# Centring-only LayerNorm with the deviation applied at eviction, and three changes of order, in a fused attention and MLP block

## The chip, the cores and the metric

The kernel runs on one core of one Trainium2 chip. The metric is the device time of one execution in microseconds (us), as a median over runs. The profile is taken on one such execution. Its time base is the "span", which runs from the first instruction to the end of the program; the device time is 1.7 to 2.0 us longer than the span in these runs. All runs of this study are in the fast state, with a granted TensorE clock between 0.998 and 1.000.

The engines are named as the profile names them: PE is TensorE (matmuls), PEld its weight loads, DVE is VectorE, ACT is ScalarE, POOL is GpSimd, and SP issues most of the DMAs.

## The reference

```python
# x: 2048 x 576, bf16; wqkv: 576 x 1728; wo: 576 x 576; w1: 576 x 4608; w2: 4608 x 576
def _layernorm(x, axis=-1, eps=1e-5):
    m = jnp.mean(x, axis=axis, keepdims=True)
    v = jnp.var(x, axis=axis, keepdims=True)
    return (x - m) / jnp.sqrt(v + eps)

# attention: 32 heads of 18; each row looks at 8 rows, two apart, ending at itself
h  = x + A(_layernorm(x), wqkv, wo)
h2 = h + gelu(_layernorm(h) @ w1 + b1) @ w2 + b2
```

What matters for this change is that the rows of a LayerNorm can be scaled after a matmul as well as before it: `((x - m) * rstd) @ W` is `((x - m) @ W) * rstd`, because `rstd` is one number for each row.

## The kernel before

The 2048 rows are 16 tiles of 128 rows. The even tiles are projected first. One projection of one tile onto Q, K or V is a "duo": a phase 0 of 10 matmuls and a phase 1 of 8, each of 64 rows by 288 columns. A "visit" does two duos (three where an output projection joins), and 24 visits do all of QKV. Attention itself is elementwise work on DVE. Then eight groups of two tiles go through MLP1 (GELU on ACT, straight out of PSUM) and MLP2. From the third group on, MLP2 uses sums of blocks of its two operands (made on DVE) to save matmuls.

Some words are used throughout. PSUM is the memory that PE writes; a "PSUM pair" is a buffer in it that ACT or DVE must empty (the "eviction") before PE may use it again. "Fillers" are matmuls whose results nobody uses, run before the first data have come. A "halo reload" reads K or V back from DRAM, shifted by rows, into `kv_ring`. `oT` is attention's output, `hnT` the second LayerNorm's output, both transposed by DMA through the buffer `td`; `w2b_sb` is the last part of `w2`.

The first LayerNorm of an even tile: statistics on DVE, the power on POOL, then the normalised tile on DVE. Only then can PE transpose it.

```python
def ln_stats(srcs, tag, c1, c0, bufs, first=None):
    # ... bn_stats on two halves, bn_aggr
    veps = sb.tile([P, n], F32, tag=f"{tag}_veps", name=f"{tag}_veps", bufs=bufs)
    nc.vector.tensor_scalar(out=veps[:], in0=mv[:, :, 1], scalar1=c1, scalar2=c0, op0=ALU.mult, op1=ALU.add)
    return mv, veps

def ln_rstd(veps, tag, bufs):
    rstd = sb.tile([P, n], F32, tag=f"{tag}_rstd", name=f"{tag}_rstd", bufs=bufs)
    nc.gpsimd.tensor_tensor(out=rstd[:], in0=veps[:], in1=mhalf[:].to_broadcast([P, n]), op=ALU.pow)
    return rstd
# ... cut: each group of tiles has a tag of its own here (ln1_0 to ln1_10), so no buffer is shared

def visit(makes, hook=None, between=(), early=False):
    duos, marks = [], []
    for make in makes:
        duos.append(make())
        marks.append(marker(phase(duos[-1], 0, None)))
        if hook and len(duos) == (1 if early else len(makes)):
            hook()                       # the transposes of the next two tiles
    for duo, mark in zip(duos, marks):
        phase(duo, 1, mark)
        duo["evac"]()                    # ACT empties the PSUM pair
        if duo is duos[0]:
            for fn in between:
                fn()

# ... cut: the eviction of a duo
pace[0] = nc.scalar.copy(out=dst..., in_=ps...).ins

# order of the start; after[v] is what the other engines are given after visit v
after = {
    0: [c_(ln1_sr, 3), c_(ln1_apply, 2), c_(ln1_apply, 3)],
    1: [c_(ln1_sr, 4), c_(ln1_sr, 5), c_(ln1_apply, 4), c_(ln1_apply, 5)],
    2: [c_(ln1_sr, 6), c_(ln1_sr, 7), c_(ln1_apply, 6), c_(ln1_apply, 7)],
    3: [c_(ln1_stats, 8)],               # statistics of the first four odd tiles
    # ... cut

# the first group: mid[0] runs between the two phases 1 of MLP1's first visit
mid[0] = [c_(exps, d)]                   # exp on ACT, between two table loads
ia[0] = [c_(wo_visit, (c, "B"))]         # first output projection, before MLP2's first row
ia[12] = [c_(exps, e), c_(wo_visit, (d, "A")), c_(ln2_pair, c, d, (e,)), ...]
```

## Time and profile before

| | before |
|---|---|
| median of the runs, four sets of rounds | 369.19 to 369.36 us |
| span of the profiled execution | 366.9 us |
| PE busy | 359.4 us, 98% |
| first QKV projection on PE | 7.38 us |
| statistics of the odd tiles start on DVE | 18.05 us |
| first MLP1 of group 1, of group 2, of group 8 | 69.32, 109.24, 329.66 us |

One caution for all that follows: the profiled execution of before took 368.69 us, which is about 0.6 us less than the medians. Every "lead" against this trace is therefore probably a little too small; leads of two changed kernels against each other are not touched by that.

The page of before. The first lines give the busy time of each engine and its share of the span; the second block is the busy share in tenths in 40 equal slices.

```profile
span 366.9 us, 11419 instructions
PE 359.4 (98%) x4900; PEld 295.5 (81%) x4900; DVE 299.3 (82%) x414; ACT 230.4 (63%) x514; POOL 41.3 (11%) x47
...
PE   8999999999999999999999999999999999999996
...
DVE  5899999999999999999989999989995699520331
...
PEclk9999999999999999999999999999999999999999
```

PE is full from the second slice on, and DVE is nearly full until about 275 us. The Trainium skill, page "Perfetto Trace Analysis", section "Identifying the Most-Contended Engine", says that the busy share of matmuls is not a good measure of how close PE is to its limit, because pipelined instructions look smaller. Here, too, the 98% doesn't show what the change can win. The list of PE's waits does: who was waited for, us in total, how often, and the longest.

```profile
PE busy L750 <- DVE prod L743: 1.5, 1, 1.5
PE po L557 <- ACT h_all L538: 0.8, 1, 0.8
PE pm L215 <- ACT h_all L538: 0.5, 1, 0.5
PE o_pt L182 <- DVE h L449: 0.4, 1, 0.4
PE po L642 <- DVE h_all L622: 0.2, 1, 0.2
PE pq L215 <- ACT kv_ring L301: 0.2, 1, 0.2
```

The first line only delays fillers. The next four are what parts 2 and 3 of the change aim at: ACT's GELUs before MLP2 (0.8) and in MLP1 (0.5), DVE's `h` before a transpose (0.4), a block sum of the last group (0.2). Together they are 1.9 us, and this is about the size of what can be won after the start.

The timeline of ACT in before, around the wait of 0.5 us: start, duration, engine, line, operation and tiles, and how many in a row.

```profile
73.31 0.84 ACT L538 ACTIVATE h_all<-pm,b_sb 128x256 bf16<-128x256 f32 x2
74.17 1.28 ACT L371 ACT_TABLE_LOAD   x1
75.47 0.42 ACT L371 ACTIVATE logits<-logits 128x256 f32<-128x256 f32 x1
75.90 1.28 ACT L514 ACT_TABLE_LOAD   x1
77.19 0.20 ACT L514 ACTIVATE warm<-mhalf 128x1 f32<-128x1 f32 x1
```

The exp takes 0.42 us, but with two table loads it keeps ACT from GELU, and so from emptying PSUM, from 74.17 to 77.39 us. For the later comparison, the timeline of DVE in before where the start ends:

```profile
17.50 0.41 DVE L166 TENSOR_SCALAR q_all<-x_all,ln_mv,ln_rstd 128x512 bf16<-128x512 bf16 x1 [0.22 <-POOL ln_rstd L162]
17.83 0.31 DVE L166 TENSOR_SCALAR xn_tail<-x_all,ln_mv,ln_rstd 128x128 bf16<-128x128 bf16 x1
18.05 0.81 DVE L151 BATCH_NORM_STATS2 ln_stats<-x_all 128x6 f32<-128x288 bf16 x2
```

In brackets stands the idle time before an instruction and what ended it. At 18.05 us DVE begins the statistics of the odd tiles.

### The profile page before, as it was taken

The numbers are of one execution on the slowest core, as the hardware profiler recorded it, in microseconds if no ns is written. First come the engines' busy times: TensorE is split into PE (matmuls) and PEld (weight loads), VectorE is DVE, ScalarE is ACT, GpSimd is POOL, SyncE is SP. The second block draws the span as 40 slices with busy tenths as digits, with TensorE's granted clock in tenths as the row PEclk, the third lists the DMA queues.
The fourth block names the chain that finished last, engine by engine and source line by source line (L and its number), as shares of the span: only waits on it lengthen the run. The fifth ranks groups of instructions, "written<-read, shape, count | busy, mean of one in ns | idle before, by whom it ended". The sixth has DMA issues, their size and how long they took to land.

```text
span 366.9 us, 11419 instructions
## 1 busy us (share of the span) xinstructions
PE 359.4 (98%) x4900; PEld 295.5 (81%) x4900; DVE 299.3 (82%) x414; ACT 230.4 (63%) x514; POOL 41.3 (11%) x47
## 2 busy tenths in 40 slices
PE   8999999999999999999999999999999999999996
PEld 3789877888778877887788778877887788779974
DVE  5899999999999999999989999989995699520331
ACT  2688755798638673568546865685568556726620
POOL 2322004000220031002100111011101010100000
PEclk9999999999999999999999999999999999999999
DMA  7989798954557625520553145305520452030001
GB/s 237 317 224 269 186 208 224 333 195 71 179 152 155 229 83 101 126 48 34 136 106 69 36 122 110 77 32 133 107 54 33 89 102 38 2 90 18 2 2 33
DMA packets 61891, 43.70 MB, mean 119 GB/s; under 512 B 31872, under 2 KB 60160, under 8 KB 61840
## 3 DMA queue, kind: packets, MB, share of 16 engines
q1 hardware_dynamic: 59952, 41.13, 41.2%
q0 software_dynamic: 1728, 1.77, 4.6%
q8 instruction: 38, 0.62, 0.7%
q10 hardware_dynamic: 160, 0.07, 0.1%
q14 instruction: 13, 0.11, 0.1%
HBM read 21.10 MB, written 12.42 MB: 91 GB/s over the span
## 4 chain that ended last, share of the span: by engine, by line
PE 78%; DVE 11%; ACT 6%; issue 1%; DMA 1%; POOL 1%; SPq 1%; DVEq 0%
PE pm L215 37%; PE po L642 22%; PE po L557 10%; PE pw L215 4%; PE pq L215 4%; ACT h_all L538 3%; DVE ln_stats L151 2%; DVE prod L339 2%; DVE prod L385 1%; DVE prod L333 1%; PE busy L750 1%; DMA hnT<-td 1%; DVE prod L391 1%; POOL ln_rstd L162 1%; DVE ln_mv L152 1%
## 5 line engine op out<-in xcount | busy, mean ns | idle before, releaser
L538 ACT ACTIVATE h_all<-pm,b_sb 128x256 f16<-128x256 f32 (+1 forms) x288 | 108.5, 498 | 73.2 <-PE pm L215 73.2
L215 PE MATMUL pm<-hnT,w_sb 64*128 64x256 bf16 x2304 | 143.0, 269 | 0.6 <-ACT h_all L538 0.5
L215 PEld LDWEIGHTS <-w_sb 64*128 64x128 bf16 x2304 | 114.2, 94 | 13.6 <-issue 2.5
L642 PEld LDWEIGHTS <-h_all 128*128 128x128 f16 x544 | 52.2, 98 | 15.8 <-issue 2.5
L215 PE MATMUL pq<-wq_sb,xnT 64*128 64x288 bf16 x768 | 54.2, 283 | 0.3 <-ACT kv_ring L301 0.2
L215 PEld LDWEIGHTS <-xnT 64*128 64x128 bf16 x864 | 43.9, 94 | 9.2 <-ACT xnT L262 0.6
L339 DVE TENSOR_TENSOR prod<-prod 128x2304 bf16<-128x2304 bf16 (+1 forms) x64 | 44.2, 691 | 2.1
L642 PE MATMUL po<-w2a_sb,h_all 128*128 128x288 bf16 (+1 forms) x312 | 43.6, 286 | 0.2 <-DVE h_all L622 0.2
L385 DVE TENSOR_TENSOR prod<-kv_ring,probs 128x4608 bf16<-128x4608 bf16 x16 | 40.9, 2555 | 2.4 <-DMA kv_ring<-kv_dram 2.1
L333 DVE TENSOR_TENSOR prod<-kv_ring,q_all 128x4608 bf16<-128x4608 bf16 x16 | 40.8, 2549 | 0.2
L215 PE MATMUL pm<-hnT,w1h_sb 64*128 64x256 bf16 x288 | 39.6, 269 | 0.0
L465 POOL TENSOR_TENSOR ln_rstd<-ln_var,mhalf 128x1 f32<-128x1 f32 x14 | 16.4, 1172 | 183.7 <-ACT ln_var L464 183.7
L557 PEld LDWEIGHTS <-h_all 128*128 128x128 bf16 x288 | 27.8, 98 | 8.8 <-issue 1.9
L391 DVE TENSOR_TENSOR prod<-prod 128x2304 bf16<-128x2304 bf16 (+1 forms) x32 | 33.8, 1057 | 1.0
L557 PE MATMUL po<-w2a_sb,h_all 128*128 128x288 bf16 x224 | 28.6, 286 | 0.8 <-ACT h_all L538 0.8
L642 PEld LDWEIGHTS <-kv_ring 128*128 128x128 f16 x240 | 23.4, 98 | 6.3 <-DVE kv_ring L622 0.4
L301 ACT CAST kv_ring<-pq 128x576 bf16<-128x576 f32 x32 | 19.4, 641 | 8.3 <-PE pq L215 8.2
L642 PE MATMUL po<-w2b_sb,h_all 128*128 128x288 bf16 (+1 forms) x152 | 22.2, 286 | 0.0
L622 DVE TENSOR_TENSOR kv_ring<-h_all 128x1536 f16<-128x1536 f16 (+2 forms) x8 | 6.6, 820 | 16.3 <-ACT h_all L538 16.3
L215 PE MATMUL pw<-wo_sb,oT 64*128 64x288 bf16 x256 | 19.5, 283 | 0.0
L162 POOL TENSOR_TENSOR ln_rstd<-ln_veps,mhalf 128x1 f32<-128x1 f32 (+2 forms) x13 | 13.2, 1019 | 49.0 <-DVE ln_veps L156 42.4
L449 DVE TENSOR_TENSOR h<-pw,x_all 128x576 f32<-128x576 f32 x16 | 11.5, 752 | 7.7 <-PE pw L215 7.7
(97 smaller groups left out, 370.7 us busy)
## 6 DMA issues: line engine op xcount, KB each, us to landing
w_sb<-in_B_w_dram SPq DMA_DIRECT2D x6, 768.0 KB, 5.6
kv_ring<-kv_dram SPq DMA_DIRECT2D x28, 144.0 KB, 2.7
w2a_sb<-in_B_w_dram SPq DMA_DIRECT2D x4, 1008.0 KB, 6.3
kv_dram<-kv_ring SPq DMA_DIRECT2D x13, 288.0 KB, 4.4
out_dram<-o_sb SPq DMA_DIRECT2D x15, 144.0 KB, 2.9
td<-q_all SPq DMA_DIRECT2D x14, 144.0 KB, 2.5
td<-hn SPq DMA_DIRECT2D x14, 144.0 KB, 1.8
x_all<-in_A_x_dram SPq DMA_DIRECT2D x12, 144.0 KB, 2.7
```

The costliest lines, as they stand in the source:

```text
L162: nc.gpsimd.tensor_tensor(out=rstd[:], in0=veps[:], in1=mhalf[:].to_broadcast([P, n]), op=ALU.pow)
L215: last = nc.tensor.matmul(duo["g"][r ^ swap][i], lhsT=lhsT, rhs=rhs, start=(swap == 0 and i == 0 and kt == 0), stop=(swap == 1 and kt == K ...
L301: pace[0] = nc.scalar.copy(out=dst.rearrange("p (d g h) -> p g d h", g=2, h=H // 2), in_=ps[:, :, 0:HALF].rearrange("p g (h d) -> p g d h" ...
L333: nc.vector.tensor_tensor(out=prod[:], in0=k_ring[j % 2], in1=q_all[:, j, :].unsqueeze(1) .to_broadcast([P, W, D]), op=ALU.mult)
L339: nc.vector.tensor_tensor(out=prod[:, :, o * H:o * H + n], in0=prod[:, :, a * H:a * H + n], in1=prod[:, :, c * H:c * H + n], op=ALU.add)
L385: nc.vector.tensor_tensor(out=prod[:].rearrange("p w (d h) -> p w d h", h=H), in0=v_ring[j % 2].rearrange("p w (d h) -> p w d h", h=H), in ...
L391: nc.vector.tensor_tensor(out=prod[:, 0:n, :], in0=prod[:, 0:n, :], in1=prod[:, n:2 * n, :], op=ALU.add)
L449: nc.vector.tensor_tensor(out=h[:].rearrange("p (g c) -> p g c", g=2), in0=pw[:, :, 0:HALF], in1=x_of(j).rearrange("p (g c) -> p g c", g=2 ...
L465: nc.gpsimd.tensor_tensor(out=rstd[:], in0=var[:], in1=mhalf[:], op=ALU.pow)
L538: pace[0] = nc.scalar.activation(out=hT(grp)[:, f, 0:N], in_=ps[:, r, i * N:(i + 1) * N], func=ACT.Gelu_apprx_tanh, bias=b1_sb[:, f:f + 1] ...
L557: nc.tensor.matmul(banks[half], lhsT=hT(grp)[:, f, i * P:(i + 1) * P], rhs=w2_rows(f)[:, half * HALF:(half + 1) * HALF], start=(f == 0), s ...
L642: nc.tensor.matmul(bank, lhsT=l, rhs=r, start=start, stop=stop, skip_group_check=True)
```

## The change

The intent has three parts.

1. **Start.** An even tile is only centred (one subtraction) before its transposes; `rstd` is computed later and handed to ACT as the scale of the PSUM eviction. The statistics of the second tile go to ACT. Fillers run on a constant, so that they need not wait for DVE. The transposes of two tiles, which stood together in a visit, are split: one tile behind each duo. The `eps` step of the even tiles gets one shared tag with two buffers. V's weights are loaded in two pieces, and their last rows through ACT's queue; the copy of one transposed tile goes from ACT to DVE.
2. **MLP1 of the first group.** The exp goes behind the second duo; the last visit empties the PSUM pair that MLP2 needs first; the first output projection moves into MLP1; one transpose of attention's output moves one phase later.
3. **Last groups.** The last LN2 is shared between ACT (one tile) and DVE (the other), and the block sums of `h` are made in pieces, the first of them during MLP1.

```diff
-    def visit(makes, hook=None, between=(), early=False):
+    def visit(makes, hook=None, between=(), late=None):
 ... a hook or a between may now be a dict {after which duo: functions}; late is a duo begun inside the last phase 1
-                pace[0] = nc.scalar.copy(out=..., in_=...).ins
+                scale = dict(scale=rstd_of[j]) if j in EVEN else {}
+                pace[0] = nc.scalar.activation(out=..., in_=..., func=ACT.Copy, **scale).ins
 ...
-            load_wqkv_half(nc.scalar, slice(1, 2))
+            load_wqkv_half((nc.scalar, nc.scalar), slice(1, 3))
-            load_wqkv(2)
-            load_wqkv_half(nc.sync, slice(2, 3))
+            load_wqkv(2, 0, 2)
+            load_wqkv(2, 2, KF)
-        for n in [512] * 9 + [P] * 5:
-            nc.tensor.matmul(busy[:, 0, 0:n], lhsT=prod[:, 0, 0:P], rhs=prod[:, 0, 0:n], start=True, stop=True)
+        ones = nc.const_aps.tensor(1.0, [P, 512], BF16)
+        for n in [512] * 8 + [P] * 5:
+            nc.tensor.matmul(busy[:, 0, 0:n], lhsT=ones[:, 0:P], rhs=ones[:, 0:n], start=True, stop=True)
 ...
+        def ln1_even(gi):
+            mv, veps = ln1[gi] = ln_stats([x_all[:, EVEN[gi], :]], f"ln1_{gi}", 1.0, EPS, 1, None, False)
+            center(EVEN[gi], mv[:, 0, 0:1], ALU.subtract)
+        def ln1_even_act(gi):            # second tile: two accumulating passes on ACT
 ...
+        def ln1_even_rstd(*gis):
+            for gi in gis:
+                mv, var = ln1.pop(gi)
+                veps = qp.tile([P, 1], F32, tag="ln1_veps", name="ln1_veps", bufs=2)
+                nc.vector.tensor_scalar(out=veps[:], ...)
+                rstd_of[EVEN[gi]] = ln_rstd(veps, f"ln1_{gi}", 1)[:, 0:1]
 ...
-            0: [c_(ln1_sr, 3), c_(ln1_apply, 2), c_(ln1_apply, 3)],
-            1: [c_(ln1_sr, 4), c_(ln1_sr, 5), c_(ln1_apply, 4), c_(ln1_apply, 5)],
-            2: [c_(ln1_sr, 6), c_(ln1_sr, 7), c_(ln1_apply, 6), c_(ln1_apply, 7)],
-            3: [c_(ln1_stats, 8)],
+            0: [c_(ln1_even, 3), c_(ln1_even, 4)],
+            1: [c_(ln1_even_rstd, 2, 3), c_(ln1_even, 5)],
+            2: [c_(ln1_even, 6), c_(ln1_even, 7), c_(ln1_even_rstd, 4, 5)],
+            3: [c_(ln1_even_rstd, 6, 7), c_(ln1_stats, 8)],
 ...
-            18: [c_(tr_o, A[1], "D")],
+            18: {1: [c_(tr_o, A[1], "D")]},
-                mid[0] = [c_(exps, d)]
+                mid[0] = {1: [c_(exps, d)]}
-                ia[0] = [c_(wo_visit, (c, "B"))]
+                late_wo = wo_duo(c, "B")
 ...
-                x["h"] += [c_(h_sums, SR, NM, (0, 2)), c_(h_sums, SR, NM, (1, 3))]
+                mid[3] = {1: [c_(h_sums, SR, 16)]}
+                x["h"] += [c_(h_sums, 16, NM)]
 ... and in group 7, ln2 of one tile on ACT, of the other on DVE
```

More of the change, by code (lines that the diff above doesn't have):

```diff
@@ L114, in load_wqkv, with load_wqkv_half @@
              A_wqkv[k0 * P:k1 * P, t * D:(t + 1) * D].rearrange("(k p) c -> p k c", p=P))
-    def load_wqkv_half(engine, ts):
+    def load_wqkv_half(engines, ts):
         src = A_wqkv[KF * P:D, :].rearrange("p (t g c) -> p t g c", t=3, g=2)
         for r in range(2):
-            engine.dma_start(out=wqh_sb[half_rows(r), ts, :], in_=src[:, ts, r, :])
+            engines[r].dma_start(out=wqh_sb[half_rows(r), ts, :], in_=src[:, ts, r, :])
     def load_wo(qs):
@@ L141, in load_w2, with ln_stats @@
         load(dst, B_w2[f0 * P:f1 * P, :].rearrange("(ft p) c -> p ft c", p=P))
-    def ln_stats(srcs, tag, c1, c0, bufs, first=None):
+    def ln_stats(srcs, tag, c1, c0, bufs, first=None, eps=True):
         n = len(srcs)
@@ L154, in ln_stats @@
                 first()
+        if not eps:
+            return mv, None
         veps = sb.tile([P, n], F32, tag=f"{tag}_veps", name=f"{tag}_veps", bufs=bufs)
@@ L227, in marker, with first @@
         return nop
-    def visit(makes, hook=None, between=(), early=False):
+    def visit(makes, hook=None, between=(), late=None):
         duos, marks = [], []
-        for make in makes:
+        def first(make):
             duos.append(make())
             marks.append(marker(phase(duos[-1], 0, None)))
-            if hook and len(duos) == (1 if early else len(makes)):
+        for make in makes:
+            first(make)
+            if hook and not isinstance(hook, dict) and len(duos) == len(makes):
                 hook()
-        for duo, mark in zip(duos, marks):
-            phase(duo, 1, mark)
-            duo["evac"]()
-            if duo is duos[0]:
-                for fn in between:
-                    fn()
+            elif isinstance(hook, dict) and len(duos) in hook:
+                hook[len(duos)]()
+        for n in range(len(makes) + (late is not None)):
+            if late is not None and n == len(makes) - 1:
+                first(late)
+            phase(duos[n], 1, marks[n])
+            duos[n]["evac"]()
+            for fn in (between.get(n, ()) if isinstance(between, dict) else between if n == 0 else ()):
+                fn()
     xnT, xn_tail = {}, {}
@@ L252, in tr_x @@
     def tr_x(js, tag):
-        pair = psum_pair(tag, "xt_pt", BF16)
+        pair = psum_pair(tag or "CAB"[(ring_pos[0] + 1) % 3], "xt_pt", BF16)
         for n, j in enumerate(js):
@@ L261, in copy @@
                 for k0, k1 in ((0, 2), (2, KT)) if j == EVEN[0] else ((0, KT),):
-                    nc.scalar.copy(out=xnT[j][:, k0:k1], in_=tr_view(pair, n)[:, k0:k1])
+                    copy = nc.vector.tensor_copy if j == EVEN[1] else nc.scalar.copy
+                    copy(out=xnT[j][:, k0:k1], in_=tr_view(pair, n)[:, k0:k1])
             copies.append(copy)
@@ L300, in evac @@
                 dst = (q_all[:, j, :], k_ring[j % 2][:, j // 2, :], v_ring[j % 2][:, j // 2, :])[t]
-                pace[0] = nc.scalar.copy(out=dst.rearrange("p (d g h) -> p g d h", g=2, h=H // 2),
-                                         in_=ps[:, :, 0:HALF].rearrange("p g (h d) -> p g d h", h=H // 2)).ins
+                scale = dict(scale=rstd_of[j]) if j in EVEN else {}
+                pace[0] = nc.scalar.activation(out=dst.rearrange("p (d g h) -> p g d h", g=2, h=H // 2),
+                                               in_=ps[:, :, 0:HALF].rearrange("p g (h d) -> p g d h", h=H // 2),
+                                               func=ACT.Copy, **scale).ins
                 if j == ATT_ORDER[0] and t > 0:
@@ L454, in ln2, with ln2_more @@
     def ln2(j):
-        h = ln2_h(j)
+        ln2_h(j)
+        ln2_more(j)
+    def ln2_more(j):
+        h = h_of[j]
         hn[j] = (h,) + ln_stats([h[:]], "ln2", 1.0 + EPS, EPS * EPS, 2)
@@ L472, in ln2_send, with ln2_out @@
         hn[j] = dma_out(y[:])
+    def ln2_out(j):
+        hn[j] = dma_out(hn[j][:])
     read = [None]
@@ L727 @@
     with tc.manual_schedule(engines={ENG.PE, ENG.Activation, ENG.DVE, ENG.SP, ENG.Pool}):
-        for i in range(2):
-            load_x(EVEN[i:i + 1])
+        load_x(EVEN[0:1])
+        load_x(EVEN[1:2])
         load_wqkv(1, 0, 2)
         load_wqkv(1, 2, KF)
-        load_wqkv_half(nc.scalar, slice(1, 2))
+        load_wqkv_half((nc.scalar, nc.scalar), slice(1, 3))
         load_x(EVEN[2:3])
         load_x(EVEN[3:4])
-        load_wqkv(2)
-        load_wqkv_half(nc.sync, slice(2, 3))
+        load_wqkv(2, 0, 2)
+        load_wqkv(2, 2, KF)
         load_x(EVEN[4:6])
@@ L740 @@
         load_wqkv(0)
-        load_wqkv_half(nc.sync, slice(0, 1))
+        load_wqkv_half((nc.sync, nc.sync), slice(0, 1))
         load_x(ODD[4:8])
@@ L762, in ln1_rstd @@
             ln1[gi] += (ln_rstd(ln1[gi][1], f"ln1_{gi}", 1),)
-        def ln1_apply(gi):
-            mv, _, rstd = ln1.pop(gi)
-            for i, j in enumerate(ln1_groups[gi]):
-                if j not in EVEN[5:]:
-                    ln_apply(q_all[:, j, :], x_all[:, j, :], mv[:, i, 0:1], rstd[:, i:i + 1])
-                    continue
-                ln_apply(q_all[:, j, 0:KF * P], x_all[:, j, 0:KF * P], mv[:, i, 0:1], rstd[:, i:i + 1])
-                xn_tail[j] = qp.tile([P, 2, HP], BF16, tag="xn_tail", name="xn_tail", bufs=3)
-                ln_apply(xn_tail[j][:], x_all[:, j, KF * P:D].unsqueeze(1).to_broadcast([P, 2, HP]),
-                         mv[:, i, 0:1], rstd[:, i:i + 1])
+        rstd_of = {}
@@ new lines, in center @@
+        def center(j, mean, op):
+            nc.vector.tensor_scalar(out=q_all[:, j, 0:D if j in EVEN[:5] else KF * P],
+                                    in0=x_all[:, j, 0:D if j in EVEN[:5] else KF * P], scalar1=mean, scalar2=None, op0=op)
+            if j in EVEN[5:]:
+                xn_tail[j] = qp.tile([P, 2, HP], BF16, tag="xn_tail", name="xn_tail", bufs=3)
+                nc.vector.tensor_scalar(out=xn_tail[j][:], in0=x_all[:, j, KF * P:D].unsqueeze(1).to_broadcast([P, 2, HP]),
+                                        scalar1=mean, scalar2=None, op0=op)
@@ new lines, in ln1_even @@
+        def ln1_even(gi):
+            mv, veps = ln1[gi] = ln_stats([x_all[:, EVEN[gi], :]], f"ln1_{gi}", 1.0, EPS, 1, None, False)
+            center(EVEN[gi], mv[:, 0, 0:1], ALU.subtract)
+        def ln1_even_act(gi):
+            j = EVEN[gi]
+            junk = q_all[:, ODD[-1], :]
+            nmean, var = (qp.tile([P, 1], F32, name=f"ln1_{t}") for t in ("nmean", "sq"))
+            nc.scalar.activation(out=junk, in_=x_all[:, j, :], func=ACT.Identity, scale=-1.0 / D, accum_out=nmean[:])
+            nc.scalar.activation(out=junk, in_=x_all[:, j, :], func=ACT.Square, bias=nmean[:], accum_out=var[:])
+            center(j, nmean[:], ALU.add)
+            ln1[gi] = (None, var)
@@ L775, in ln1_sr @@
+        def ln1_even_rstd(*gis):
+            for gi in gis:
+                mv, var = ln1.pop(gi)
+                veps = qp.tile([P, 1], F32, tag="ln1_veps", name="ln1_veps", bufs=2)
+                nc.vector.tensor_scalar(out=veps[:], in0=var[:] if mv is None else mv[:, 0, 1:2],
+                                        scalar1=1.0 / D if mv is None else 1.0, scalar2=EPS, op0=ALU.mult, op1=ALU.add)
+                rstd_of[EVEN[gi]] = ln_rstd(veps, f"ln1_{gi}", 1)[:, 0:1]
         def ln1_sr(gi):
@@ L789, in ln1_act @@
             ln_apply_act(q_all[:, j, :], x_all[:, j, :], rstd[:, i:i + 1], nmr[:, i:i + 1])
-        ln1_sr(0)
-        ln1_sr(1)
-        ln1_apply(0)
-        ln1_apply(1)
-        ln1_sr(2)
+        ln1_even(0)
+        ln1_even_act(1)
         A = ATT_ORDER
@@ L817, in ln2_stats @@
             for j in (c, d):
-                (add_b2 if c == GROUPS[-1][0] else put_b2)(j)
+                put_b2(j)
         def ln2_ins(c, d):
@@ L873 @@
         hooks = {
-            1: c_(tr_x, EVEN[2:4], "D"),
-            2: c_(tr_x, EVEN[4:6], "D"),
-            3: c_(tr_x, EVEN[6:8], "D"),
+            **{n: {m: c_(tr_x, EVEN[2 * n + m - 1:2 * n + m], "D" if m == 1 else None) for m in (1, 2)} for n in (1, 2, 3)},
             12: c_(tr_b1, "D"),
@@ L887 @@
         tr_x(EVEN[1:2], "C")
+        ln1_even_rstd(0, 1)
+        ln1_even(2)
         for qd in range(len(seq) // 2):
@@ L891 @@
                 duos.append(wo_duo(wo_with[qd], "D"))
-            visit(duos, hooks.get(qd), between.get(qd, ()), qd in (1, 2))
+            visit(duos, hooks.get(qd), between.get(qd, ()))
             call(after.get(qd, ()))
@@ L899, with mlp1_plan, mlp1 @@
         h_all = late.tile([P, FT, 2 * P], BF16, name="h_all")
-        def mlp1_plan(p, q, r, s, fast):
-            end = (r, s, p) if fast else (s, r, p)
+        def mlp1_plan(p, q, r, s, end):
             return [[([2 * v + n], tag) for n, tag in enumerate(tags)] for v, tags in enumerate(((p, q), (r, s), (p, q), end))]
-        def mlp1(grp, plan, ahead, between):
+        def mlp1(grp, plan, ahead, between, late=None):
             for v, duos in enumerate(plan):
                 call(ahead.get(v, ()))
-                visit([mlp1_duo(grp, us, tag) for us, tag in duos], None, between.get(v, ()))
+                visit([mlp1_duo(grp, us, tag) for us, tag in duos], None, between.get(v, ()), late if v == 3 else None)
         def mlp2_tile(grp, i, tag, inserts):
@@ L922, in exps, with wo_visit @@
             gelu_table()
-        def wo_visit(*duos):
-            visit([wo_duo(j, tag) for j, tag in duos], (lambda: [ahead[0]() for _ in range(2)]) if len(duos) == 1 else None)
+        def wo_visit(*duos, fill=False):
+            visit([wo_duo(j, tag) for j, tag in duos], (lambda: [ahead[0]() for _ in range(2)]) if fill else None)
         ROWS = {2: 8, 3: 12, 4: 12, 5: 12, 6: NM, 7: NM}
@@ L933 @@
             e, f = GROUPS[k + 2] if k + 2 < len(GROUPS) else (None, None)
-            m1, mid, ia, ib = {0: []}, {}, {}, {}
+            m1, mid, ia, ib, late_wo = {0: []}, {}, {}, {}, None
             if k in (1, 2):
@@ L938 @@
                 m1[0] += [c_(halos, 1), c_(att_qk_a, d), c_(att_qk_rest, d, 1), c_(halo, d, 1)]
-                mid[0] = [c_(exps, d)]
+                mid[0] = {1: [c_(exps, d)]}
                 m1[1] = [c_(pv_t, c), c_(pv_t, d), c_(load_w2, 4), c_(att_qk, e, 0)]
-                ia[0] = [c_(wo_visit, (c, "B"))]
-                ia[12] = [c_(exps, e), c_(wo_visit, (d, "A")), c_(ln2_pair, c, d, (e,)), c_(halos, 2), c_(send_o, e)]
+                late_wo = wo_duo(c, "B")
+                ia[12] = [c_(exps, e), lambda d=d: wo_visit((d, "A"), fill=True), c_(ln2_pair, c, d, (e,)), c_(halos, 2), c_(send_o, e)]
                 ib[0] = [c_(finish_out, g[0])]
@@ L955 @@
             if k < 2:
-                mlp1(g, mlp1_plan(p, q, r, s, False), m1, mid)
+                mlp1(g, mlp1_plan(p, q, r, s, (s, r, p) if k else (r, s, p)), m1, mid, late_wo)
                 mlp2_tile(g, 0, "D", ia)
@@ L985 @@
             if c is not None:
-                x["h"] = [c_(ln2_stats, c, d)] + x["h"]
-                x["6"] += [c_(ln2_send, c)]
-                x["7"] = [c_(ln2_send, d)] + x["7"]
+                if k == 6:
+                    x["h"] = [c_(ln2_h, c), c_(ln2_act, c), c_(ln2_h, d)] + x["h"] \
+                        + [c_(ln2_more, d), c_(ln2_rstd, d), c_(ln2_send, c), c_(add_b2, c), c_(add_b2, d), c_(ln2_bias, d)]
+                    x["6"] += [c_(ln2_hn, d), c_(ln2_out, d)]
+                else:
+                    x["h"] = [c_(ln2_stats, c, d)] + x["h"]
+                    x["6"] += [c_(ln2_send, c)]
+                    x["7"] = [c_(ln2_send, d)] + x["7"]
                 x["in"] = [c_(ln2_ins, c, d)] + x["in"]
                 wo = lambda tags: wo_visit((c, tags[0]), (d, tags[1]))
-            mlp1(g, mlp1_plan(p, q, r, s, True), m1, mid)
+            mlp1(g, mlp1_plan(p, q, r, s, (r, s, p)), m1, mid)
             mlp2_fast(g, rows, (p, q, r, s), wo, x)
```

## The prediction

> **What bounds the kernel now.** TensorE. The page's busy table gives PE 98% of the 366.9 us span; the window table gives PE 200.0 of 200 us between 110 and 310 us, and the granted clock is 1.00. The matmul stream is untouched, so only the places where PE waits or runs fillers can pay. The PE timeline and the wait list name them: before the first projection (7.38 us; fillers from 1.53 us), about 1 us inside the first QKV visit (7.38 to 10.57 us where a later visit of 36 matmuls takes 2.21 us), 0.35 us at 54.8 us (second o transpose waits for DVE's h), 0.47 us at 78.9 us (ACT was doing exp between two table loads instead of emptying a PSUM pair), 0.76 us at 89.3 us (ACT's last GELUs before MLP2), about 0.3 us at 319.5 us, 0.14 us at 329.6 us (the last hnT transpose lands exactly when PE needs it), 0.24 us at 351.5 us. DVE is the second limit: 9 tenths or more in nearly every slice until about 285 us.
>
> **The change, costed from the trace.**
> 1. Start. The rstd step (veps 0.15, POOL pow 0.55 to 0.67 us) leaves the path before the transposes; tile 0 is centred at about 4.65 us instead of 5.9. But ACT's two accumulating passes for tile 1 (estimate 1.8 us from LN2's 0.67+0.19+0.78+0.19) end near 5.8 us, and PE transposes both tiles before projecting, so I expect the first projection near 6.9 us, not 5.5. Visit 0 loses fewer bubbles. PE gains about 1.2 us by the end of the fourth visit. Wq's V part (issued at 3.9 us, 5.6 us to landing) leaves little more to win.
> 2. DVE gains much less: per tile 0.15 us of veps moves rather than disappears, the pow waits (1.3 us in all) go, tile 1's statistics (1.05 us) move to ACT, but one PSUM copy (estimate 0.7 us) comes. Net lead about 0.4 us. DVE runs without a gap to 54 us and beyond, so PE's lead is cut there: the DVE lead plus 0.5 us from transposing o one phase later.
> 3. MLP1 of the first pair: exp later and pair D emptied first remove 0.47+0.76 us. Part is lost again, because the second output projection (93.0 us) waits for an oT that lands near 92.2 us and moves only with DVE. Lead carried into the next stage: about 1.2 us.
> 4. Group 6: block sums of the late rows need no waiting (0.3 us), hnT about 1 us earlier (0.14 us). Group 7: 0.25 us.
>
> Sum: 1.2+0.4+0.3, about 1.9 us of 369.2.
>
> **Predicted: 367.2 us, 80% range 365.6 to 368.6.** Faster by over 2%: 0.015; within 2%: 0.975; slower by over 2%: 0.01.
>
> **What would show it right or wrong.** First L215 projection at 6.6 to 7.1 us; fourth visit ending 1 to 1.5 us earlier; DVE's statistics of the odd tiles (18.05 us) starting only 0.1 to 0.9 us earlier; no PE wait at MLP1's third visit nor before the first MLP2; a new PE wait at the second output projection or at the o transpose; the stages from 110 to 310 us of unchanged length; in the last group the wait on h_all gone.
>
> **What would make it wrong.** "TensorE: Matmul & The Clock Gate", Part 1, says a cold array runs at half rate for about 3.4 us of activity; the trace agrees (fillers of 512 columns 0.427 us apart at first). Fewer fillers and gaps between the first transposes could leave PE cold longer, costing up to 1 us. If DVE leads by more than I think, the gain reaches 3 us; if it does not lead at all, only 1 us remains.

## The result and the profile after

| | before | after |
|---|---|---|
| median of 6 runs | 369.19 us | 367.50 us |
| lowest and highest | 368.72, 369.59 | 367.02, 368.27 |
| span of the profiled execution | 366.9 us | 366.1 us |

The ratio is 0.9956, with a 95% interval of 0.9942 to 0.9970: 0.44% faster. A ratio here is the mean time of one kernel's fast runs over that of the other's fast runs of the same rounds, so it is not quite the ratio of the medians quoted. Two later sets of rounds gave 0.9952 and 0.9953.

The first lines of the page of after, and then its list of PE's waits:

```profile
span 366.1 us, 11432 instructions
...
PE 358.8 (98%) x4899; PEld 292.4 (80%) x4899; DVE 299.8 (82%) x425; ACT 231.6 (63%) x511; POOL 40.9 (11%) x47
```

```profile
PE pw L217 <- DMA oT<-td: 1.3, 1, 1.3
PE busy L770 <- PEq L1050: 0.8, 1, 0.8
PE pq L217 <- DMA wq_sb<-in_A_wqkv_dram: 0.6, 2, 0.4
PE po L661 <- DVE kv_ring L641: 0.4, 1, 0.4
PE pq L217 <- ACT q_all L312: 0.2, 1, 0.2
```

All five of the old waits on work (ACT twice, DVE twice, and the PSUM pair of QKV) are gone. In their place stand a wait of 1.3 us for `oT` (attention's output, transposed by DMA for the second output projection), 0.6 us for QKV weights, 0.4 us for a block sum and 0.2 us for an eviction on ACT.

The exp block in after, again from ACT's timeline, lies 1 us later. It takes as long as before, but the PSUM pair that PE wanted next has been emptied by then:

```profile
74.27 0.87 ACT L557 ACTIVATE h_all<-pm,b_sb 128x256 bf16<-128x256 f32 x2
75.16 1.28 ACT L383 ACT_TABLE_LOAD   x1
76.45 0.42 ACT L383 ACTIVATE logits<-logits 128x256 f32<-128x256 f32 x1
```

How far PE is ahead of before's trace at fixed events tells where the time came from. In us, negative is earlier; the three columns of after are three profiled executions of the same kernel, two of them from later rounds:

| event on PE (time in before) | after | after, 2nd | after, 3rd |
|---|---|---|---|
| first QKV projection (7.38) | -1.08 | -1.13 | -1.11 |
| first MLP1 of group 1 (69.32) | -0.47 | -0.63 | -0.95 |
| first MLP2 of group 1 (89.27) | -1.54 | -1.51 | -1.94 |
| first MLP1 of group 2 (109.24) | -0.82 | -0.99 | -1.38 |
| first MLP1 of group 4 (183.95) | -0.81 | -0.98 | -1.38 |
| first MLP1 of group 5 (220.44) | -0.27 | -0.98 | -1.38 |
| first MLP1 of group 8 (329.66) | -0.77 | -1.48 | -1.87 |
| last matmuls (362.82) | -1.19 | -1.89 | -2.29 |
| span (366.9) | -0.8 | -1.5 | -1.9 |

Three things stand out. First, of the lead of 1.1 us at the first projection only 0.47, 0.63 and 0.95 us are left when MLP1 begins. Second, the first execution lost 0.54 us between groups 4 and 5, and the others did not: a halo reload issued at 183.05 us landed at about 189.0 us, DVE waited 2.50 us for it, and a block sum came 0.37 us too late for PE. The two other executions of the same kernel show that this doesn't come with the change each time (one more trace, `three_edits` below, has a wait of 2.12 us at the same place). Third, the lead at the end of the span is 0.4 us less than at the last matmuls, in all three.

DVE's timeline where the start ends, in after:

```profile
16.56 0.21 DVE L811 TENSOR_SCALAR ln_veps<-ln_mv 128x1 f32<-128x1 f32 x2
17.37 0.15 DVE L811 TENSOR_SCALAR ln_veps<-ln_mv 128x1 f32<-128x1 f32 x1 [0.60 <-POOL ln_rstd L164]
17.88 0.15 DVE L811 TENSOR_SCALAR ln_veps<-ln_mv 128x1 f32<-128x1 f32 x1 [0.36 <-POOL ln_rstd L164]
17.95 0.81 DVE L151 BATCH_NORM_STATS2 ln_stats<-x_all 128x6 f32<-128x288 bf16 x2
```

DVE reaches the four small `veps` at 16.56 us. It writes two, then waits 0.60 and 0.36 us: there are two buffers, and the third write needs POOL's power to have read the first. So the statistics of the odd tiles start at 17.95 us, 0.10 us earlier than before, though their turn came at about 16.8 us. The chain of waits of after names where this lands (start, duration, what):

```profile
17.88 0.15 DVE ln_veps L811
18.04 0.74 DVE ln_stats L151 x2
...
21.82 0.18 DVE ln_veps L158
22.00 0.07 issue
22.07 1.03 POOL ln_rstd L164
23.10 0.02 issue
23.13 0.17 DVE ln_nmr L173
23.30 0.02 issue
23.32 0.87 ACT q_all L177
24.19 0.64 ACT q_all L312
24.83 0.04 issue
24.87 1.14 PE pq L217 x15
```

It is read from top to bottom: DVE's last `veps`, the odd statistics, POOL's power, the bias, ACT's normalisation of an odd tile (0.87 us, ahead of the eviction in ACT's order), then the eviction, then PE, which had waited 0.20 us.

### The profile page after: what moved, and what is told of

It is laid out like the page before. It is cut to its first block, busy times and chain, and to the rows that moved or that the text cites. A ratio compares the mean times of both kernels' runs of the same rounds, so it can differ in the third digit from the quotient of the medians.

```text
span 366.1 us, 11432 instructions
## 1 busy us (share of the span) xinstructions
PE 358.8 (98%) x4899; PEld 292.4 (80%) x4899; DVE 299.8 (82%) x425; ACT 231.6 (63%) x511; POOL 40.9 (11%) x47
## 4 chain that ended last, share of the span: by engine, by line
PE 72%; DVE 18%; DMA 5%; issue 2%; POOL 1%; ACT 0%; ACTq 0%; SPq 0%; POOLq 0%; DVEq 0%
PE pm L217 29%; PE po L661 21%; PE po L576 9%; PE pq L217 9%; PE pw L217 4%; DVE prod L397 3%; DVE prod L351 3%; DVE prod L345 2%; DVE prod L403 2%; DMA kv_ring<-kv_dram 2%; DVE ln_stats L151 2%; DMA x_all<-in_A_x_dram 1%; DMA wqh_sb<-in_A_wqkv_dram 1%; DVE kv_ring L641 1%; POOL ln_rstd L164 1%
## 5 line engine op out<-in xcount | busy, mean ns | idle before, releaser
L217 PEld LDWEIGHTS <-w_sb 64*128 64x128 bf16 x2304 | 111.7, 94 | 15.0 <-issue 1.7
L641 DVE TENSOR_TENSOR kv_ring<-h_all 128x1536 f16<-128x1536 f16 (+3 forms) x10 | 6.9, 687 | 15.9 <-ACT h_all L557 15.9
L217 PEld LDWEIGHTS <-oT 64*128 64x128 bf16 x288 | 13.4, 94 | 6.3 <-DMA oT<-td 1.7
L730 ACT COPY po<-po 128x288 f32<-128x288 f32 x18 | 6.9, 385 | 14.6 <-PE po L661 11.4
```

Of the source, the lines that this page charges most:

```text
L217: last = nc.tensor.matmul(duo["g"][r ^ swap][i], lhsT=lhsT, rhs=rhs, start=(swap == 0 and i == 0 and kt == 0), stop=(swap == 1 and kt == K ...
L641: nc.vector.tensor_tensor(out=s_slot(t, m0, m1), in0=a, in1=b, op=alu)
```

## Theories and experiments

The question of the experiments: the total is near the prediction, but in this trace the start's 1.1 us are gone soon: 0.07 us are left on PE at the first transpose of attention's output (47.73 us before), and DVE is 0.10 us ahead at the odd tiles. Why?

**Theory 1.** DVE carries the lead of the start to the later stages, and loses it at the shared two-buffer tile. With as many buffers as tiles, the statistics of the odd tiles start over 1 us earlier, the chain above starts earlier, and PE keeps what it won.

**The rival (Theory 2).** The loss is not in DVE's wait. It is on ACT, where evictions now carry a scale and take longer, or in the loads of the start; more buffers change nothing, cheaper evictions do.

A second question came with the parts: what does the new wait for `oT` cost, and can it be taken away?

### The change once more, and its parts

`after_again` is the changed kernel without any edit. `start_only` keeps part 1 and undoes 2 and 3; `mlp_only` and `last_only` are the kernel before with part 2 or part 3 alone. The edit of `start_only`, in short:

```diff
-            18: {1: [c_(tr_o, A[1], "D")]},
+            18: [c_(tr_o, A[1], "D")],
-                mid[0] = {1: [c_(exps, d)]}
+                mid[0] = [c_(exps, d)]
-                late_wo = wo_duo(c, "B")
+                ia[0] = [lambda c=c: wo_visit((c, "B"), fill=True)]
-                mid[3] = {1: [c_(h_sums, SR, 16)]}
-                x["h"] += [c_(h_sums, 16, NM)]
+                x["h"] += [c_(h_sums, SR, NM, (0, 2)), c_(h_sums, SR, NM, (1, 3))]
 ... the order of MLP1's last pairs and the last LN2 as before
```

`mlp_only` and `last_only` add the same lines to the kernel before, with the part of `visit` that they need.

> The changed kernel once more, on the chip of the three partial kernels. Both theories: ratio to before 0.994 to 0.997 (about 1.7 us). If the 2.5 us in which DVE waited near 187 us for the reload of a ring (before: 0.67 us) is an accident of one execution's DMA, this profile shows less than 1.5 us there and the matmul stream enters the sixth group of tiles about 0.5 us further ahead; if the change causes it, it is there again.

> Only the start of the change (centring, deviation at eviction, ACT statistics, fillers, loads, pieces of the transposes); the MLP1 part and the last group as before. Theory 1 (the start is paid for by DVE, whose lead at the odd tiles' statistics is only 0.1 us): the first projection comes 1.1 us earlier, but PE is at most 0.2 us ahead at 48 us, waits for h at the o transpose again, and the kernel gains 0.0 to 0.4 us (ratio 0.999 to 1.000). Theory 2 (the start's gain of about 1 us is carried by PE to the end): gain 0.9 to 1.3 us, ratio 0.9965 to 0.9975.

> Only the o transpose one phase later, exp later, and the first output projection inside MLP1. Theory 1 (the waits it removes are partly given back to an oT that only DVE can bring earlier): the waits of 0.47 and 0.76 us are gone, a new wait of 0.7 to 1.0 us stands before the second output projection, and the gain is 0.7 to 0.9 us (ratio about 0.998). Theory 2 (removed waits add up): gain 1.5 us, ratio 0.996.

> Only the last LN2 on two engines and the block sums in pieces. Both theories: nothing changes before 310 us, 0.4 us from the seventh group and 0.3 to 0.4 us from the eighth, ratio about 0.998. If instead the last group's second step is bounded by something else (a DMA), less than 0.4 us in all.

| kernel | median us | ratio to before | 95% interval |
|---|---|---|---|
| before (11 runs) | 369.32 | | |
| after_again | 367.43 | 0.9952 | 0.9940 to 0.9963 |
| start_only | 369.04 | 0.9996 | 0.9985 to 1.0008 |
| mlp_only | 368.13 | 0.9970 | 0.9958 to 0.9982 |
| last_only | 368.06 | 0.9969 | 0.9957 to 0.9981 |

The largest part of the change by lines of code is worth nothing that can be told from zero, and the two smaller ones are worth about 1.1 us each. By ratios the parts sum to 0.65%, the whole is 0.48%; with intervals of about 0.12% on each, the difference lies inside the noise.

In the trace of `mlp_only` the waits of 0.8 and 0.5 us for ACT and the 0.4 us for `h` are gone and a wait of 1.2 us for `oT` is new. Its ratio of 0.9970 lies between the two that had been expected (0.998 if part is given back, 0.996 if the waits add up), so it doesn't decide between them. In that of `start_only` all old waits of the later stages are still there, and the one for `h` has grown from 0.4 to 0.6 us: what PE had won, DVE had not. In `last_only` PE gained 0.50 us in group 7 and 0.41 us in group 8; in that execution it was already 0.7 us behind before at its first MLP1 (70.04 us), in code that it shares with before. Some 0.4 us of this were lost at the second visit, where PE waited for the weights of V (0.25 us are named at 10.22 us).

### More buffers for one small tile: veps8

```diff
-                veps = qp.tile([P, 1], F32, tag="ln1_veps", name="ln1_veps", bufs=2)
+                veps = qp.tile([P, 1], F32, tag="ln1_veps", name="ln1_veps", bufs=8)
```

Each buffer is 4 bytes in a partition.

> The changed kernel with eight buffers instead of two for the variance plus eps, so that DVE need not wait for POOL's power before it writes the next one (0.60 and 0.36 us at 17.4 and 17.9 us). Theory 1 (DVE carries the start's gain, and this wait ate it): the odd tiles' statistics start 0.8 to 1.0 us earlier than in the changed kernel, PE is 0.4 us or more ahead of before at the first o transpose (changed kernel: 0.07 to 0.23), the wait before the second output projection shrinks from 1.1 to 1.3 us to under 0.8, the second pair's MLP1 starts 1.5 to 1.9 us ahead of before (changed kernel: 0.82 to 0.99), and the kernel gains 0.6 to 0.9 us on the changed one: ratio to before 0.9925 to 0.9940. Theory 2 (the weight loads or ACT's longer evictions ate it): no change, ratio 0.995 to 0.9955.

Measured: 366.99 us, ratio 0.9932 (0.9919 to 0.9944) where `after_again`, in another call, has 0.9952 (0.9940 to 0.9963). The statistics of the odd tiles started at 16.66 us, 1.29 us earlier than in after. But in this execution part of the lead was gone by the second transpose of attention's output: DVE waited 0.80 us (33.18) and 0.62 us (49.01) for halo reloads, and PE then 0.6 us for DVE's `h`. The first MLP1 of group 2 came only 0.75 us ahead of before, where 1.5 us or more had been expected. The intervals still overlapped a little, and the trace showed the first step of Theory 1 but not the whole way.

### The same again, and with the start alone: veps8_again, start_veps8, after_third

The three were run together on another chip, with before at 369.34 us. `after_third` is the changed kernel unedited, `veps8_again` is `veps8`, and `start_veps8` is `start_only` with eight buffers.

> The changed kernel a third time, as the partner on one chip of the two kernels with eight buffers. Ratio 0.9945 to 0.9960; PE 0.0 to 0.3 us ahead of before at the first o transpose.

> Eight buffers for the variance plus eps, again. The first run was 0.5 to 0.7 us faster than the changed kernel by the clock, while its profiled execution lost DVE's lead again to two late reloads of the rings (0.80 and 0.62 us). Theory 1: ratio 0.0012 to 0.0025 below that of the changed kernel in this call; the odd tiles' statistics start about 1 us earlier than in it; if the reloads come in time, PE is 0.4 us or more ahead of before at both o transposes. Rival: the first difference was noise between chips: ratio within 0.001 of the changed kernel's.

> Only the start of the change, with eight buffers; MLP1 and the last group as before. The start alone gave 0.9996. Theory 1 (two buffers made DVE give the gain back): now 0.5 to 0.9 us faster than before, ratio 0.9975 to 0.9987, with DVE's statistics of the odd tiles about 1.2 us earlier than before. Rival (the start is worth nothing whatever DVE does, because reloads and weight loads come next): ratio 0.999 or higher.

| kernel | median us | ratio to before | 95% interval |
|---|---|---|---|
| after_third | 367.60 | 0.9953 | 0.9940 to 0.9966 |
| veps8_again | 366.49 | 0.9928 | 0.9917 to 0.9940 |
| start_veps8 | 368.06 | 0.9972 | 0.9960 to 0.9984 |

The start alone goes from 0.9996 to 0.9972 by this one number: about 0.9 us. (The two ratios: each against before of its own rounds.) In the whole change it is worth 0.20% and 0.25%; the fast runs of `veps8_again` average 366.62 us and those of `after_third` 367.52 us. One expectation failed: `after_third` was 0.54 us ahead of before at the first transpose of attention's output, where 0.0 to 0.3 us had been expected. It too lost 0.39 us in visit 7, but had come there with more. DVE's timeline of `veps8_again` at the same place:

```profile
16.15 0.33 DVE L811 TENSOR_SCALAR ln_veps<-ln_mv 128x1 f32<-128x1 f32 x4
16.40 0.81 DVE L151 BATCH_NORM_STATS2 ln_stats<-x_all 128x6 f32<-128x288 bf16 x2
```

The four writes go through in 0.33 us, and the statistics follow at 16.40 us.

The visits of QKV show the spot on PE. The table gives the lead over before in us near the end of phase 0 (the last two of its ten matmuls), in visits 6 and 7 counted from 1; between the two lies the eviction that the chain of waits above ends in.

| | visit 6, second duo (23.24) | visit 7, second duo (25.44) | lost |
|---|---|---|---|
| after | 0.45 | 0.09 | 0.36 |
| after_again | 0.63 | 0.25 | 0.38 |
| after_third | 0.95 | 0.56 | 0.39 |
| start_only | 0.52 | 0.18 | 0.34 |
| row18 (below) | 0.47 | 0.12 | 0.35 |
| veps8 | 0.67 | 0.66 | 0.01 |
| veps8_again | 0.90 | 0.89 | 0.01 |
| start_veps8 | 0.69 | 0.68 | 0.01 |
| both (below) | 0.17 | 0.17 | 0.00 |
| three_edits (below) | 0.01 | 0.01 | 0.00 |

All five profiled executions with two buffers (and the right result) lose 0.34 to 0.39 us there, and all five with eight buffers lose at most 0.01 us. How much lead there was to lose differs between executions, 0.01 to 0.95 us at visit 6; the loads of the start are the likely reason, but no run tested them. In `start_veps8` the lead is 0.67 us at the first transpose of attention's output, 1.07 us at the first MLP1 and still 1.00 us at the last matmuls; in `start_only` it is 0.15, -0.11 and 0.08 us. Theory 1 holds for the device time: the two-buffer tile takes most of what the start can gain (0.9 us), first on PE in visit 7 and then, in `start_only`, through a DVE that is hardly earlier than before, at the second transpose of attention's output, where PE waits 0.6 us for `h`.

### Evictions without the scale: noscale

This kernel gives a wrong result on purpose (relative error 0.69): the even tiles are never multiplied by `rstd`.

```diff
-                scale = dict(scale=rstd_of[j]) if j in EVEN else {}
+                scale = {}
```

> The changed kernel without the scale at the eviction of the even tiles: wrong results on purpose. It takes away ACT's longer evictions (1.37 us for two instead of 1.18) and ACT's wait for POOL. Theory 1 (DVE): PE's lead over before at the first o transpose and at the second pair's MLP1 stays within 0.2 us of the changed kernel's (0.07 to 0.23, and 0.82 to 0.99); ratio as the changed kernel's. Theory 2 (ACT's evictions ate the start's gain): the lead at the first o transpose is 0.4 us or more and the ratio 0.001 lower.

Measured: 367.21 us, ratio 0.9943 (0.9928 to 0.9957), not to be told from the changed kernel's 0.9952 and 0.9953. The trace can't be set beside that of after: x's third tile came without the wait that after had (its statistics at 7.03 us, 7.52 in after), so all of the start was earlier (odd statistics at 17.40 us), and PE's lead at the first transpose of attention's output was 0.73 us, far from what Theory 1 had said (0.43 us at most). `after_third` had an early third tile too (6.77 us), odd statistics at 17.48 us and a lead of 0.54 us there. What can be read is the same step in visit 7: `noscale` lost 0.27 us there, where the kernels with the scale and two buffers lost 0.34 to 0.39. So of the loss about 0.1 us belongs to the scale, an estimate from that one execution. It fits the evictions themselves, from ACT's timelines of before and of after:

```profile
24.20 1.16 ACT L301 CAST q_all<-pq 128x576 bf16<-128x576 f32 x2
```

```profile
24.10 1.35 ACT L312 ACTIVATE q_all<-pq,ln_rstd 128x576 bf16<-128x576 f32 x2
```

Two evictions take 1.35 instead of 1.16 us, which is 0.095 us more for each (in after the evictions of odd tiles, without a scale, still take 0.64 to 0.65 us one by one, and those with a scale 0.72 to 0.74). The Trainium skill, page "ScalarE: Activation LUTs", section "What ACT_TABLE_LOAD costs", gives about 93 ns for each operand that is a pointer to one value per partition; the trace agrees. The rival's mechanism is real, then, and small: eight buffers remove the whole loss with the scale in place.

### The wait for oT: row18 and both

The second output projection is inserted after 12 rows of MLP2; moving it to row 18 lets `oT` land first. `both` has this and the eight buffers.

```diff
-                ia[12] = [c_(exps, e), lambda d=d: wo_visit((d, "A"), fill=True), ...]
+                ia[18] = [c_(exps, e), lambda d=d: wo_visit((d, "A"), fill=True), ...]
```

> The changed kernel with the second output projection of the first pair six rows of MLP2 later, so that PE works instead of waiting for oT (1.1 to 1.3 us). Theory 1 (only DVE can bring the next stage earlier): the wait goes, but a wait for the transposed LN2 result appears at the start of the second pair's MLP1, which starts only 0.2 to 0.5 us earlier than in the changed kernel; gain on it 0.2 to 0.5 us. Theory 2 (the wait itself is the loss): the gain is the whole 1.1 to 1.3 us, ratio near 0.992.

> Both edits. Theory 1: DVE's lead of about 1 us brings the transposed LN2 result earlier too, so the second pair's MLP1 starts 2.0 to 2.4 us ahead of before, without a long wait, and the kernel is 1.1 to 1.4 us faster than the changed one: ratio 0.9915 to 0.9925. Theory 2 (effects of the two edits overlap, PE lost elsewhere): no better than the better of the two single edits.

Measured: `row18` 367.39 us, 0.9955 (0.9943 to 0.9967), no gain, which neither theory had expected; `both` 366.56 us, 0.9925 (0.9911 to 0.9940), the same as `veps8` within the noise. The first line of PE's waits in `row18`:

```profile
PE po L576 <- DMA w2b_sb<-in_B_w_dram: 1.8, 1, 1.8
```

The wait for `oT` is gone and another of 1.8 us has taken its place. PE now reaches the rows of MLP2 that need `w2b_sb` at 96.3 us and must wait until 98.11 us; that load is issued at 90.6 us behind the transpose of `oT` and took 7.5 us to land. In after it landed at about 96.7 us and was used at 97.5 us. The two deadlines lie so close that removing one wait only uncovers the other. `both` still waits 1.24 us for this load.

### The weight load issued earlier: three_edits

`both`, and in addition the load of `w2b_sb` issued ahead of attention's products instead of behind them (75.2 us instead of 90.6).

```diff
-                m1[1] = [c_(pv_t, c), c_(pv_t, d), c_(load_w2, 4), c_(att_qk, e, 0)]
+                m1[1] = [c_(load_w2, 4), c_(pv_t, c), c_(pv_t, d), c_(att_qk, e, 0)]
```

> Eight buffers, the second output projection six rows later, and the last part of W2 asked for before the two transposes of o instead of behind them: the six rows alone only moved the wait (1.8 us) to that load. Theory: no wait of PE over 0.5 us between 85 and 100 us; the second pair's MLP1 starts 1.6 to 2.3 us ahead of before (changed kernel 0.8 to 1.0), unless its LN2 result is late; ratio 0.9905 to 0.9925. If the earlier load delays the transposes of o instead, a wait of 0.5 us or more for oT is there and the ratio is that of eight buffers alone or worse.

Measured: 368.78 us (367.19 to 369.35), ratio 0.9976 (0.9959 to 0.9993): worse than `veps8_again` of the same rounds, by 0.48%. PE's waits in its trace:

```profile
PE pm L217 <- DMA hnT<-td: 1.4, 1, 1.4
PE pw L217 <- DMA oT<-td: 1.1, 1, 1.1
```

The load was in flight for 7.9 us, from 75.2 to 83.2 us. In that time attention's first output was stored (issued at 80.33 us), and its transpose could be issued only 3.9 us after that; in after it followed its store (80.96) by 1.6 us. So the *first* output projection now waited 1.1 us, DVE waited 6.9 us in all for halo reloads (3.6 in after, 2.5 of it in the one wait told above), and PE waited 1.4 us for the transposes of the next LN2. The Trainium skill, page "DMA: Bandwidth & Descriptors", section "Issuing engines are not separate DMA queues", says that all DMAs run on the same 16 engines and interleave. This trace fits that: a load moved out of the way of one transfer was in the way of another. That the load did it, and not the later row or a mishap of the execution, is argued from the times of issue and landing and not tested alone.

### The end of the span

The last two DMA issues, from SP's timelines of before and of after:

```profile
364.00 0.33 SPq L677 DMA_DIRECT2D out_dram<-o_sb  x1
```

```profile
362.81 0.33 SPq L696 DMA_DIRECT2D out_dram<-o_sb  x1
```

From this last store to the end of the span before takes 2.9 us (364.00 to 366.9) and after 3.3 us (362.81 to 366.1). The store lands after 1.6 us in both. With the span taken unrounded from the traces, before shows 2.89 us and after 3.28; all ten other traces of kernels with the changed start show 3.27 to 3.29 us, and those of `mlp_only` and `last_only`, which have the old start, 2.90 and 2.89 us. So the changed start costs about 0.38 us at the very end of the program, after the last landing.

The timelines don't list what runs there, but the packed traces have it: SP goes through a row of semaphore waits that end the program. The three kernels with the old start do seven of them, 0.06 to 0.08 us apart. All eleven with the changed start do eight, and between two of these 0.37 or 0.38 us pass instead of 0.07. So the cost is one wait more and one pause of about 0.3 us. What makes the pause, and which line of part 1 does it, no run tells. This stays open.

## Why the prediction was right or wrong

The prediction of 367.2 us was right: 367.50 us were measured, and later 367.43 and 367.60. The class (within 2%) was right as well. Some terms of the sum were wrong, and they offset one another; that the total came out so near is in part luck.

- **What bounds the kernel, and which waits pay: right.** The stages from group 2 to group 6 kept their length in two of three traces to 0.01 us; the exception is the late reload told above. All gains came from the places that the prediction lists.
- **First projection "near 6.9 us": too late.** It came at 6.30 us. The centring of the second tile needs only the first of ACT's two passes (ended 5.02 us, centring at 5.06); the second pass, which gives the variance, lies beside the path.
- **"PE gains about 1.2 us by the end of the fourth visit": the term that was mis-sized.** Read near the end of phase 0 of visit 5's first duo, the first point after the fourth visit's work, it is 0.06 us in after, and 0.25 and 0.57 us in its two other traces; at the second duo of visit 5 it is 0.44, 0.63 and 0.94 us. The lead of 1.08 us at the first projection shrinks in after as follows. (a) PE waits for QKV weights: 0.38 us are named in the waits at 7.11 us, and the weights of V cost another 0.3 us or so, read from a group of 24 matmuls that takes 1.97 us instead of 1.63. (b) Splitting the transposes costs PE time that the prediction did not see. In before and after alike, the next projection starts 0.12 us after the start of the last one, but a transpose 0.21 us after it: going over costs about 0.1 us. Coming back costs about 0.1 us more only where the transposes end with a 128-row piece (`xn_tail`, used for three tiles): the last transpose is followed after 0.05 us by another transpose in before, and after 0.15 us by a projection. Where they end with a 64-row piece it is 0.17 us either way. Now there are two such pairs of switches in a visit instead of one. This fits what is lost: measured at the first duo of visits 2 to 5, the lead falls by 0.12, 0.12 and 0.21 us from one to the next in after, and by the same to 0.01 us in `veps8`. (c) About 0.38 us come back between the two duos of visit 5, where before waited for a PSUM pair and after doesn't. Points (a) and (b) are read from traces; no run undid them alone.
- **"Net lead about 0.4 us" on DVE: wrong step, and a size that is right by luck.** The prediction said that "the pow waits (1.3 us in all) go" and priced the moved `veps` at 0.15 us each. It did not see that they share a tile with two buffers, so that POOL's wait comes back: 0.60 + 0.36 us. The lead was 0.10 us, and 0.26 and 0.57 us in the two other traces; with eight buffers, where those waits are gone as the prediction had it, it was 0.85 to 1.65 us. So the rest of the step had been priced too low. This is shown by `veps8`, `veps8_again` and `start_veps8`. The slower eviction (0.095 us each) was missed as well.
- **"PE's lead is cut there" (by DVE, near 54 us): right in kind, at another place.** It was cut already in visit 7 (25 us), through DVE, POOL and ACT's evictions, by 0.36 to 0.39 us in the three traces. At the first transpose of attention's output 0.07, 0.23 and 0.54 us were left, and no trace of after has a wait of PE for `h`; those of `start_only` and `veps8` have one, of 0.6 us in each.
- **MLP1 of the first group: right in kind.** The waits of 0.47 and 0.76 us are gone, and so is the 0.35 us for `h`. The new wait for `oT` was foreseen and is 1.35 us. The lead into group 2 was predicted as 1.2 us and is 0.82, 0.99 and 1.38 us.
- **Last groups: 0.44 us predicted for group 7, 0.50 measured; 0.25 for group 8, 0.42 measured.** The wait of 0.24 us for `h_all` is gone. But about 0.38 us are given back behind the last store, by a cost at the end of the span that the prediction did not know.
- **The clock risk did not come true.** The prediction cites the page "TensorE: Matmul & The Clock Gate", Part 1: a cold array runs at half rate for about 3.4 us of activity. After starts its fillers at 0.78 us, 0.75 us earlier than before, and its first projections run at the same rate as before's (eight matmuls in 0.67 and 0.66 us).

So the sum of 1.9 us was right because the last groups gave a little more than was said, while the start gave next to nothing (`start_only` 0.9996) and MLP1's part made up for it (`mlp_only` 0.9970, about 1.1 us). Had one only looked at the total, the two-buffer tile would have stayed in.

Best of all kernels that give the right result are the changed one with eight buffers (366.99 and 366.49 us, 0.9932 and 0.9928) and `both` (366.56 us, 0.9925), which cannot be told apart. The first is a change of one number and beats both the kernel before and the changed kernel.

## What to carry to other kernels

When small values that one engine writes and another reads move from tags of their own to a shared tag, count the buffers against how many are written in a row: with too few, the waits that a reordering was meant to remove come back under another name. Follow a gain at the start to the engine that carries it further, and check that this engine, too, is earlier; a lead on the busiest engine alone shrank from 1.10 to 0.18 us within 20 us here (`start_only`). A wait for a DMA that is removed by moving its consumer or another load often uncovers the next transfer's deadline, so read the slack of the neighbouring transfers (here 0.8 us) before counting the wait as a gain.

## What the Trainium skill lacked or had wrong

- "ScalarE: Activation LUTs", section "What ACT_TABLE_LOAD costs": it gives about 1.28 us for a table load and about 2.66 us in all with a drain for every switch. Here the load takes 1.28 us, but from the start of the load to the start of the exp pass 1.30 us (74.17 to 75.47 us), and the load starts 0.02 us after the last GELU ends (74.15). No further 1.38 us show in this trace.
- "GPSIMD Engine Reference" has no figure for a power on a small tile. On 128x1, each of the eight in after's start took 0.55 us, and two in a row (16.79 to 17.85 us) were enough to hold up DVE for 0.96 us where two buffers are shared; one on 128x4 took 1.02 us. Later ones on 128x1 took 0.55 to 2.8 us.
- "TensorE: Matmul & The Clock Gate": no page gives a time for a switch between 64-row projections and 128-row transposes. Here it costs PE about 0.1 us to go over, and to come back 0.1 us or nothing, depending on the last transpose.
- "Runtime: NRT & Kernel Launch" lists the runtime's steps around a kernel, but no page has the semaphore waits with which this program itself ends: 1.3 to 1.7 us from the last landing to the end of the span, seven or eight waits of about 0.07 us at first, nor why a changed start should add one of them and a pause of 0.3 us.
